# Asking for V on ScalarE's queue, and reading three weight operands in quarters

## Chip, cores and metric

The kernel runs on one core of a Trainium2 chip. The metric is the device time of one execution in microseconds; the figure for a kernel is the median of several runs. A profile is one execution recorded by the hardware profiler. Its span is the time from the first to the last recorded instruction.

The engines are called as in the profile: PE is TensorE (PEld its weight loads), DVE is VectorE, ACT is ScalarE, POOL is GpSimd, SP is SyncE. SPq and ACTq are instructions that the sequencers of SP and ScalarE carry out themselves, above all the issuing of DMAs.

## What is computed

A layer norm feeds two branches: attention over the last 512 positions of a cached K and V, and a gated feed-forward net. The result is `x + s * silu(ffn)`. Cut to what matters, with the shapes filled in:

```python
# x: (1, 2048, 640)   k_cache, v_cache: (1, 32, 2048, 192)   wq: (640, 6144)   wo: (6144, 640)
# w_gate, w_up: (640, 1536)   w_down: (1536, 640)            all bfloat16
def A(xn):                                   # 32 heads of 192, window W = 512
    q = (xn @ wq).reshape(1, 2048, 32, 192).transpose(0, 2, 1, 3)
    k, v = k_cache[:, :, -512:], v_cache[:, :, -512:]
    p = softmax(einsum("bhqd,bhkd->bhqk", q, k) * 192 ** -0.5)
    o = einsum("bhqk,bhkd->bhqd", p, v)
    return o.transpose(0, 2, 1, 3).reshape(1, 2048, 6144) @ wo

def B(xn):
    return (silu(xn @ w_gate) * (xn @ w_up)) @ w_down

xn = layernorm(x)                            # eps 1e-5
return x + A(xn) * silu(B(xn))
```

## The kernel before

It runs in three stages. **The feed-forward net** (0 to about 172 us) works on four blocks of 512 rows. It leaves `silu(B)` in DRAM (`g_d`), and beside it differences of blocks of `wo` (`wo_d`) that the last stage needs. **The attention** (to about 700 us) goes through the 32 heads in 16 pairs, numbered 0 to 15. **The output projection** (to the end) multiplies the attention's output by `wo` in two by two blocks with seven products in place of eight, M1 to M7. Each product needs one weight operand of 1.92 MB, held in a tile `b_w`. M1 and M2 use blocks of `wo` as they are; M7 uses a difference from `wo_d`; `B_SUMS` lists the products whose operands are such differences.

**One pair of heads.** All tiles of the attention hold two heads, one in the lower and one in the upper 64 rows of TensorE. A pair goes through the four blocks of 512 query rows in two halves. Each half is a `scores_phase` and a `stretch`.

- `scores_phase(pr, half)` runs eight steps, n from 0 to 7 in the first half and 8 to 15 in the second. Step n does what `slots` lists for it, then `scores` (six matmuls into a PSUM tile `sc`, and on ScalarE the `exp` that writes the probabilities `p_t`), then `beside(pr, n)`. The slots hold the projection of the queries that are needed next: `differences` ahead of the first scores, `sides` ahead of the second, `across` and `third(0)` ahead of the fourth, `sums` ahead of the fifth, `third(1)` ahead of the seventh, and in the first half `q_diag` ahead of the eighth. `sides` ends with a copy of its PSUM bank to `m_f` on ScalarE; `third(0)` writes into that same bank.
- `stretch(pr, half)` multiplies the probabilities of the half with V (`pv`, 128 matmuls at L689) and divides by the sums (`divide`, on VectorE and ScalarE). After each of four units SP issues a DMA transpose of the result (`OT_b`). `spill` writes these to DRAM in the next half.

The order on each engine is the order of the program, written out by hand: the kernel runs under a manual schedule, and each engine and each DMA queue takes its work as the code names it.

**Loads around a pair.** `beside(pr, n)` places them:

- n = 0: the transpose of the next pair's K by DMA (`transpose_k`, on SP), then `load_v(pr)`, two DMAs of 192 KB on SP, one for each head. They fill `V_p`, of which there is one copy: it can be written once the matmuls of the pair before have read it, and the first `stretch` of this pair needs it.
- n = 10 and 12: the projection weights and K of the pair after next (`load_wq`, `load_k`, on SP).
- n = 4, 5, 12, 13: `spill` of the half before, on SP.
- whatever the table `AHEAD` holds for `(pr, n)`: mostly operands of the output projection, fetched while there is time. `load_b` fetches a weight operand on ScalarE's queue in one DMA, M1 at (1, 10), M7 at (4, 10) and M2 at (7, 10). `wo_part` copies one more operand (M3) within DRAM, in four pieces of 480 KB on SP's queue, at (2, 7), (2, 15), (3, 7) and (3, 15).

`KH` is 24, the number of 128-row chunks of an operand; `pre` is the pool that holds the operands fetched early.

Of the kernel before, what the change touches and what calls it, by code (L numbers as in the profile page):

```python
# [15 lines left out]
def kernel(  # L16
# [13 lines left out]
    nc = tc.nc  # L30
# [20 lines left out]
    KH = NPAIR * PD // P // 2  # L51
# [4 lines left out]
    bf = dt.bfloat16  # L56
# [42 lines left out]
    M1, M7, M2, M5, M6, M4, M3 = PRODUCTS = range(10, 17)  # L99
# [9 lines left out]
    B_SUMS = [m for m in PRODUCTS if len(B_OF[m]) == 2]  # L109
# [3 lines left out]
    wo_d = dram.tile([len(B_SUMS) + 1, P, KH, HC], h16, name="wo_d")  # L113
# [65 lines left out]

    def load_v(pr):  # L180
        for h in range(2):
            nc.sync.dma_start(
                out=V_p[:, :, h, 0:Dh],
                in_=vv[2 * pr + h, k0:Sk, :].rearrange("(p j) d -> p j d", j=KC),
            )
# [41 lines left out]
    a_q, b_w = {}, {}  # L227

    with ExitStack() as fctx:
# [263 lines left out]
        for b in range(NB):  # L493
# [4 lines left out]
            for f in range(NF):  # L498
# [5 lines left out]
                n, phase = divmod((b - 1) * NF + f, 3)  # L504
# [59 lines left out]
    pre = ctx.enter_context(tc.tile_pool(name="out_first", bufs=1, side="right"))  # L564
# [171 lines left out]
    def b_tile(m, pool):  # L736
        return pool.tile([P, KH, HC], h16 if m in B_SUMS else bf, name="b_w", tag="b_w%d" % m)

    def wo_quarter(m, c0=0, c1=KH):
        k, n = B_OF[m][0]  # L740
        return wo[(k * KH + c0) * P : (k * KH + c1) * P, n * HC : (n + 1) * HC].rearrange(
            "(c p) d -> p c d", p=P
        )
# [2 lines left out]

        nc.sync.dma_start(out=wo_d[len(B_SUMS), :, c0:c1, :].bitcast(bf), in_=wo_quarter(M3, c0, c1))

    def load_b(m, pool=None, eng=nc.scalar):
        if m in b_w:  # L750
            pass
        elif pool is None:
            b_w[m] = xc[:, 0:3, :, :].rearrange("p s c n -> p (s c n)").rearrange("p (c d) -> p c d", d=HC)
        else:
            b_w[m] = b_tile(m, pool)[:, :, :]
        if eng is None:
            return
        if m in B_SUMS:
            src = wo_d[B_SUMS.index(m), :, :, :]
        elif m == M3:  # L760
            src = wo_d[len(B_SUMS), :, :, :].bitcast(bf)
        else:
            src = wo_quarter(m)
        eng.dma_start(out=b_w[m], in_=src)

    ROW_PAIRS = [(8 * g + r, 8 * g + 4 + r) for g in range(T // 8) for r in range(4)]

# [154 lines left out]
    def beside(pr, n):  # L922

        b, kc = divmod(n, KC)
        if pr < last:
            if n == 0:
                transpose_k(pr + 1)
            elif b == 2 and kc < 3:
                sum_k(pr + 1, kc)
            elif n >= 11:  # L930
                centre_k(pr + 1, n - 11)
        if n == 0:
            load_v(pr)
        elif pr + 2 < NPAIR and n in (10, 12):
            (load_k if n == 12 else load_wq)(pr + 2)
        half, n8 = divmod(n, 2 * KC)
        prev = pr * NB + 2 * half - 2
        if prev >= 0 and n8 in (4, 5):
            spill(prev + n8 - 4)
        if (pr, n) in AHEAD:  # L940
            what, *args = AHEAD[pr, n]
            what(*args)

    old, middle, most, new = (slice(*ends) for ends in ((0, KH - 6), (KH - 6, KH - 3), (0, KH - 3), (KH - 3, KH)))
    AHEAD = {
        (1, 10): (load_b, M1, pre), (4, 10): (load_b, M7, pre), (7, 10): (load_b, M2, pre),
        (last - 4, 10): (load_a, 0, 2), (last - 3, 10): (load_a, 0, 0),
        (last - 1, 3): (load_a, 0, 3, old), (last - 1, 6): (load_a, 0, 1, old),
        (last - 1, 9): (load_a, 1, 2), (last - 1, 14): (load_b, M5), (last, 5): (load_a, 1, 0),
        (last, 6): (load_a, 0, 3, middle), (last, 7): (load_a, 0, 1, middle),  # L950
    }

    for n in range(4):
        AHEAD[2 + n // 2, (7, 15)[n % 2]] = (wo_part, n * KH // 4, (n + 1) * KH // 4)

    def scores_phase(pr, half):

# [30 lines left out]
    for q in (3, 1):  # L988
        load_a(1, q, most, nc.scalar)
    load_b(M6, wide, None)  # L990
    O_last = wpool.tile([P, 2, 4, 2, Dh], bf, name="O_last", tag="wq_p")
    O_late += [O_last[:, k, :, :, :] for k in range(2)]
# [71 lines left out]
```

## Time and profile before

| | |
|---|---|
| median of 3 runs | 889.05 us (887.2 to 891.53) |
| the profiled execution | 888.36 us |
| its span | 886.6 us |
| granted TensorE clock | 1.00 |
| PE busy | 876.1 us, 99% of the span |
| PEld busy | 581.4 us, 66% |
| DVE busy | 581.4 us, 66% |
| ACT busy | 404.0 us, 46% |
| POOL busy | 113.9 us, 13% |
| DMA, mean rate | 187 GB/s, 165.50 MB |
| packets of SP's queue (q1) | 150.19 MB, 70.4% of 16 engines' span |
| packets of ScalarE's queue (q10) | 13.86 MB, 4.9% |

The shares are of the whole span, and each is an average over three stages. A line of a timeline reads: start, length (both in us from the start of the span), engine, line of the kernel, operation, tile written, tile read, number of instructions merged into the line, and in brackets how long the engine stood idle before it and what it waited for. TensorE's matmuls are pipelined, so a merged line of matmuls is longer than the distance to the next by the length of the pipeline: twelve score matmuls of 0.108 us each start within 1.29 us, and the line shows 1.48.

The issues of V, and the three loads of weight operands in the attention, before:

| transfer | queue | issues | KB each | us from issue to landing, median |
|---|---|---|---|---|
| `V_p` | SP | 32 | 192 | 3.4 |
| `b_w` from `wo` (M1, M2) | ACT | 2 | 1920 | 15.7 |
| `b_w` from `wo_d` (M7 and two later ones) | ACT | 3 | 1920 | 9.4 |
| `wo_d` from `wo` (`wo_part`) | SP | 4 | 480 | 7.0 |

### The profile page before, as it was taken

The page shows a single profiled execution, that of the slowest core. Times are in us where ns is not written, and L with a number is a line of the kernel's source. Part 1 is how long each engine was busy: PE and PEld are TensorE (multiplying, and loading weights), DVE is VectorE, ACT ScalarE, POOL GpSimd, SP SyncE. Part 2 cuts the span into 40 slices and gives each one's busy share as a digit, 9 for nine tenths or more (in the row PEclk, how much of TensorE's full clock was granted, in tenths as well). Part 3 has the DMA queues.
Part 4 walks back from the last instruction along what each step waited for, and adds up shares of the span by engine and source line. Part 5 has one row for each costly group of instructions (what it writes and reads, how often), then busy time and mean ns, then how long its engine had stood idle before and what let it go on. Part 6 is the DMA issues. An engine that isn't in the chain of part 4 may idle for free.

```text
span 886.6 us, 22883 instructions
## 1 busy us (share of the span) xinstructions
PE 876.1 (99%) x9705; PEld 581.4 (66%) x9705; DVE 581.4 (66%) x992; ACT 404.0 (46%) x577; POOL 113.9 (13%) x215
## 2 busy tenths in 40 slices
PE   9999999999999999999999999999999999999998
PEld 5455555567656766766756766766766777777775
DVE  6464766177767877777767777777776457555553
ACT  4222222465756666576666576576667400000000
POOL 0000001012132132122122122122120000000000
PEclk9999999999999999999999999999999999999999
DMA  9659775247989879869889778879799998555410
GB/s 295 175 168 254 206 214 176 66 74 170 229 189 222 181 150 254 157 143 197 204 165 205 149 142 194 181 136 239 153 192 265 249 339 313 200 193 177 173 63 16
DMA packets 272710, 165.50 MB, mean 187 GB/s; under 512 B 174048, under 2 KB 267872, under 8 KB 271968
## 3 DMA queue, kind: packets, MB, share of 16 engines
q1 hardware_dynamic: 264784, 150.19, 70.4%
q10 hardware_dynamic: 7824, 13.86, 4.9%
q8 instruction: 76, 1.25, 0.6%
q14 instruction: 26, 0.21, 0.1%
HBM read 89.95 MB, written 40.24 MB: 147 GB/s over the span
## 4 chain that ended last, share of the span: by engine, by line
PE 97%; DMA 2%; DVE 1%; issue 0%; ACTq 0%; SPq 0%
PE acc L804 21%; PE sc L650 18%; PE mm L596 13%; PE sc L372 11%; PE mm L689 10%; PE sc L689 9%; PE mm L582 8%; PE mm L393 6%; DMA V_p<-in_A_v_cache_dram 1%; PE mm L405 1%; DMA x_t<-in_A_x_dram 1%; PE gu L372 0%; DVE wq_p L174 0%; DVE qT L587 0%; ACTq L249 0%
## 5 line engine op out<-in xcount | busy, mean ns | idle before, releaser
L654 ACT ACTIVATE p_t<-sc 128x1024 bf16<-128x1024 f32 x256 | 253.7, 1024 | 59.9 <-PE sc L650 55.5
L650 PE MATMUL sc<-qT,khat 64*128 64x512 bf16 x1536 | 197.8, 376 | 0.0
L689 PEld LDWEIGHTS <-p_t 64*128 64x128 bf16 x4096 | 172.9, 94 | 14.0 <-DMA V_p<-in_A_v_cache_dram 5.1
L650 PEld LDWEIGHTS <-khat 64*128 64x128 bf16 x1536 | 89.1, 94 | 74.8
L689 PE MATMUL mm<-V_p,p_t 64*128 64x193 bf16 x2112 | 112.2, 243 | 4.3 <-DMA V_p<-in_A_v_cache_dram 4.2
L689 PE MATMUL sc<-V_p,p_t 64*128 64x193 bf16 x1984 | 104.8, 243 | 0.0
L587 DVE TENSOR_REDUCE qT<-mm 128x512 bf16<-128x1024 f32 x66 | 80.6, 1223 | 29.7 <-PE mm L582 27.2
L596 PE MATMUL mm<-xc,wq_p 64*128 64x512 f16 x750 | 94.4, 376 | 0.0
L804 PEld LDWEIGHTS <-a_s 128*128 128x128 f16 x768 | 75.1, 98 | 29.2
L596 PEld LDWEIGHTS <-wq_p 64*128 64x128 f16 (+1 forms) x1050 | 58.7, 94 | 47.6
L634 POOL TENSOR_TENSOR m_f<-m_f 128x1024 f32<-128x1024 f32 x28 | 65.9, 2352 | 178.0 <-DVE qT L629 178.0
L718 ACT ACTIVATE O_b<-sc,r 128x192 bf16<-128x192 f32 x120 | 44.0, 420 | 92.1 <-PE sc L689 84.0
L582 PE MATMUL mm<-xnT,wq_p 64*128 64x512 bf16 x660 | 82.9, 376 | 0.5 <-DVE qT L587 0.5
L804 PE MATMUL acc<-b_w,a_q 128*128 128x320 bf16 (+1 forms) x576 | 81.8, 299 | 0.0
L804 PE MATMUL acc<-b_w,a_s 128*128 128x320 f16 (+1 forms) x576 | 81.8, 299 | 0.0
L804 PEld LDWEIGHTS <-a_q 128*128 128x128 bf16 x576 | 56.3, 98 | 22.1 <-issue 0.3
L854 ACT COPY xc<-acc 128x320 f32<-128x320 f32 x8 | 3.4, 428 | 141.3 <-PE acc L804 130.8
L380 DVE TENSOR_TENSOR hT<-sc,sg 128x512 bf16<-128x512 f32 x46 | 31.6, 688 | 51.9 <-ACT sg L379 51.9
L372 PE MATMUL sc<-xnT,wg_sb 128*128 128x512 bf16 (+1 forms) x260 | 60.2, 354 | 0.5 <-issue 0.3
L582 PEld LDWEIGHTS <-wq_p 64*128 64x128 bf16 x660 | 36.2, 94 | 36.8 <-issue 5.7
L372 PE MATMUL sc<-xnT,wu_sb 128*128 128x512 bf16 (+1 forms) x260 | 60.3, 354 | 0.0
L379 ACT ACTIVATE sg<-sc 128x512 bf16<-128x512 f32 x46 | 27.3, 596 | 68.9 <-PE sc L372 67.4
(83 smaller groups left out, 863.4 us busy)
## 6 DMA issues: line engine op xcount, KB each, us to landing
o_d<-OT_b SPq DMA_DIRECT2D x64, 384.0 KB, 5.8
a_q<-o_d SPq DMA_DIRECT2D x28, 768.0 KB, 6.7
won<-in_A_wo_dram SPq DMA_DIRECT2D x24, 320.0 KB, 4.9
wo_d<-wo_s SPq DMA_DIRECT2D x12, 640.0 KB, 3.9
wq_rows<-in_A_wq_dram SPq DMA_DIRECT2D x16, 480.0 KB, 4.7
wq_rows<-in_A_wq_dram SPq DMA_DIRECT2D x30, 240.0 KB, 6.2
K_p<-in_A_k_cache_dram SPq DMA_DIRECT2D x32, 192.0 KB, 6.3
V_p<-in_A_v_cache_dram SPq DMA_DIRECT2D x32, 192.0 KB, 3.4
```

What stands on the lines that cost most here:

```text
L372: nc.tensor.matmul(out, w_sb[:, c, f * P : (f + 1) * P], xnT[:, c, qc], start=(c == 0), stop=(c == NC - 1),)
L380: nc.vector.tensor_tensor(hTs[b][:, f, :], u, sg[:], ALU.mult)
L393: nc.tensor.matmul(dn[:, n, 0:HC], hTs[b][:, f, rows], wd_sb[:, f, n * HC : (n + 1) * HC], start=(f == 0), stop=(f == NF - 1),)
L582: nc.tensor.matmul(q_ps[:, h, :], w[r, AS_IS[j], c, :], xnT[r, c, b * 512 : (b + 1) * 512], start=(c == 0), stop=(c == NC - 1),)
L587: nc.vector.reduce_sum(q_of(i, j), q_ps[:, :, :].rearrange("p h n -> p n h"), axis=AX.X)
L596: nc.tensor.matmul(ps[:, h, :], ws[h][r, c, :], xs[h][r, c, :], start=(first and c == 0), stop=(c == NC - 1), skip_group_check=True,)
L634: eng.tensor_tensor(m_f[:, SIDE_S, :, :], diag, m_f[:, SIDE_S, :, :], ALU.subtract)
L650: nc.tensor.matmul(sc[:, h, :], khat[r, j, ks], q_of(i, j)[r, :], start=(j == 0), stop=(j == 2))
L654: nc.scalar.activation(p_t[:, :, :], sc[:, :, :], ACT.Exp, scale=scale)
L689: m = nc.tensor.matmul(acc[:, k, h * 256 : h * 256 + Dh + 1], Ps[i][kc][r, h, qt * P : (qt + 1) * P], V_p[r, kc, h, 0 : Dh + 1], start=(p ...
L718: nc.scalar.activation(O_b[:, qt, h, :], a_k[:, h, 0:Dh], ACT.Copy, scale=r[:, k, h, :])
L804: nc.tensor.matmul(ps[k] if ns > 1 else ps, at[:, c, :], b_w[m][:, c, k * w : (k + 1) * w], start=(first and c == 0), stop=(c == KH - 1), ...
```

## The change

Two things change. `load_v` issues its two DMAs on ScalarE's queue. Since `beside` is called after `scores`, they stand there behind the `exp` that writes the pair's first probabilities, and ahead of the copy to `m_f`. And `load_b` takes a range of chunks: M1, M7 and M2 are each read in four pieces of six chunks (480 KB), on SP's queue, at the steps 6 and 14 of two pairs one after the other: M1 in pairs 1 and 2, M7 in pairs 4 and 5, M2 in pairs 7 and 8. The other calls of `load_b` are as before. The same bytes are moved, and the arithmetic is the same.

```diff
     def load_v(pr):
         for h in range(2):
-            nc.sync.dma_start(
+            nc.scalar.dma_start(
                 out=V_p[:, :, h, 0:Dh],
                 in_=vv[2 * pr + h, k0:Sk, :].rearrange("(p j) d -> p j d", j=KC),
             )
...
-    def load_b(m, pool=None, eng=nc.scalar):
+    def load_b(m, pool=None, eng=nc.scalar, c0=0, c1=KH):
...
         if m in B_SUMS:
-            src = wo_d[B_SUMS.index(m), :, :, :]
+            src = wo_d[B_SUMS.index(m), :, c0:c1, :]
         elif m == M3:
-            src = wo_d[len(B_SUMS), :, :, :].bitcast(bf)
+            src = wo_d[len(B_SUMS), :, c0:c1, :].bitcast(bf)
         else:
-            src = wo_quarter(m)
-        eng.dma_start(out=b_w[m], in_=src)
+            src = wo_quarter(m, c0, c1)
+        eng.dma_start(out=b_w[m][:, c0:c1, :], in_=src)
...
     AHEAD = {
-        (1, 10): (load_b, M1, pre), (4, 10): (load_b, M7, pre), (7, 10): (load_b, M2, pre),
...
     for n in range(4):
-        AHEAD[2 + n // 2, (7, 15)[n % 2]] = (wo_part, n * KH // 4, (n + 1) * KH // 4)
+        part = (n * KH // 4, (n + 1) * KH // 4)
+        AHEAD[2 + n // 2, (7, 15)[n % 2]] = (wo_part, *part)
+        for pr, m in ((1, M1), (4, M7), (7, M2)):
+            AHEAD[pr + n // 2, (6, 14)[n % 2]] = (load_b, m, pre, nc.sync, *part)
```

## The prediction

> **What bounds the kernel now.** I read the page's first two parts first (TensorE is 99% busy, the granted clock 9 in all 40 slices, that is 0.9 or more), then the chain that ended last, then the list of waits, then the timeline around the places that they name.
>
> ```profile
> PE 97%; DMA 2%; DVE 1%; issue 0%; ACTq 0%; SPq 0%
> ...
> PEld L689 <- DMA V_p<-in_A_v_cache_dram: 5.1, 3, 2.1
> ...
> PE mm L689 <- DMA V_p<-in_A_v_cache_dram: 4.2, 5, 1.6
> ```
>
> TensorE sets the time from end to end. Whatever delays its stream by x costs x; whatever delays another engine costs nothing until TensorE waits for it. The only DMA for which it waits in the attention is V, in three places. They have to be sized by the stream itself, since the two rows overlap and one place can count twice. The first matmul of a half pair (L596, `differences`) starts at 205.94, 222.96, 238.94, 258.33, 274.31, 291.33 and so on: halves that open a pair take 17.02 us, the others 15.98, to within 0.01, in all but three cases. These three take 19.39 (from 238.94), 18.57 (from 340.31) and 18.50 (from 440.87). The excess is 2.37 + 1.55 + 1.48 = **5.40 us**, all that V costs before.
>
> Why it is late there: SP's queue at the start of pair 2 (start, length, both in us).
>
> ```profile
> 237.09 10.07 SPq L721 DMA_TRANSPOSE OT_b<-O_b  x4
> 247.53 1.27 SPq L192 DMA_TRANSPOSE KT<-K_p  x1
> 248.90 1.72 SPq L182 DMA_DIRECT2D V_p<-in_A_v_cache_dram  x2
> ```
>
> V stands on SP behind four transposes of the half before and the transpose of K. In most pairs these four take 5.6 to 6.7 us, and V is asked for 5.4 us into pair 3 (279.72 against 274.31). In pairs 2, 5 and 8 they take 8.4 to 10.1 us, since `load_b` put 1.92 MB into the DMA engines at 227.81, 329.95 and 429.29, 10 to 12 us before each of these pairs. V is then asked for 9.3 to 10 us into the pair, and it is needed at 11.7 (286.00 in pair 3). The first matmul with V of pair 2 starts at 252.39, after 1.58 us of idle time put down to V.
>
> **The change, removed.** V goes past SP's five transposes and is asked for behind the first probabilities, 1.94 us into the pair (276.25 against 274.31). Landing takes 3.1 to 4.4 us in all 32 issues, and the second issue would stand at 2.7 us, so V would be there at 5.8 to 7.1, with 4.6 us to spare before 11.7. Both edits act on the same 5.40 us, which is counted once. Gain: **5.40 us**, bounds 0 (the waits stay) and 5.40.
>
> **Moved to SP.** `load_b` becomes 12 issues of 480 KB instead of three. Nearest row: `wo_part`, 480 KB on the same queue, 0.69 to 2.47 us of SP each. V's two issues (1.24 to 1.72 us) leave SP in each pair. What stands behind the pieces on SP is the transposes, K, wq and the spills. Cover: K^T is needed by VectorE at L200 in the second half, and even in pair 2, where the four transposes took 4 us longer, nothing but V stopped TensorE. The `wo_part` of 480 KB at 267.44, 282.53 and 300.98 went by with halves of 17.02 and 15.98 behind them. New is that in pair 2 a `wo_part` follows a piece directly (positions 6 and 7, 14 and 15), 960 KB, half of the load that did the harm. Taken as 0; without cover, one more late V as in pair 2, 2.4 us. The three issues that leave ScalarE (0.34 to 0.39 us each) were hidden: the probabilities after them start where they do in other pairs. 0.
>
> **Added to ScalarE.** This is the cost. The timeline of the start of pair 3 is below. Two DMA issues now stand between the first probabilities and the copy `m_f` (L626), in pairs 1 to 15. Pair 0 has another order there, with ScalarE idle 0.55 us before its second probabilities.
>
> ```profile
> 276.03 1.26 PE L596 MATMUL mm<-xnT,wq_p 64*128 64x512 bf16 x10
> ...
> 276.25 1.02 ACT L654 ACTIVATE p_t<-sc 128x1024 bf16<-128x1024 f32 x1
> ...
> 277.11 1.48 PE L650 MATMUL sc<-qT,khat 64*128 64x512 bf16 x12
> ...
> 277.38 1.01 ACT L626 COPY m_f<-mm 128x1024 f32<-128x1024 f32 x1
> ...
> 278.45 1.26 PE L582 MATMUL mm<-xnT,wq_p 64*128 64x512 bf16 x10
> ```
>
> The copy empties the bank of `sides`; `third(0)` (L582) writes that bank next. The copy ends at 277.38 + 1.01 = 278.39, `third(0)` starts at 278.45, and the scores ahead of it are through at 277.11 + 1.29 = 278.40. So TensorE has no slack at all here. Every delay of the copy moves `third(0)`, behind it the third scores, then the rest of the pair. The copy starts 1.13 us after the probabilities. What goes into this gap, by rows of ScalarE (ACTq: its DMA issues) and of SP:
>
> ```profile
> 667.64 1.02 ACT L654 ACTIVATE p_t<-sc 128x1024 bf16<-128x1024 f32 x1 [0.44 <-PE sc L650]
> 667.67 0.33 ACTq L764 DMA_DIRECT2D xc<-wo_d  x1
> ...
> 679.51 1.24 SPq L182 DMA_DIRECT2D V_p<-in_A_v_cache_dram  x2
> ...
> 712.30 0.33 ACTq L764 DMA_DIRECT2D b_w<-wo_d  x1
> 712.67 0.43 ACT L854 COPY xc<-acc 128x320 f32<-128x320 f32 x1 [10.55 <-DMA OT_b<-O_last]
> ```
>
> A DMA issue starts 0.03 us after the probabilities in front of it (667.67 against 667.64), while they run. Work behind an issue starts 0.04 us after its end (712.63 to 712.67): ScalarE keeps the order, though that copy's matmuls had ended 9 us earlier. A semaphore step adds some 0.05 us on either side (SP shows 0.09 between V's two issues). V's two issues themselves have no row on ScalarE. From below: its two `a_q` issues in a row, 684.34 to 685.20, 0.86 us. From above: V behind a K transpose on SP, 1.72 us. In between: V alone on SP in the last pair, where no K transpose precedes it, 0.575 + 0.09 + 0.575 = 1.24 us. I take that one, same bytes and same pattern; the two engines issue alike (`a_q<-o_d` at least 0.319 us on SP, 0.333 on ScalarE). Then 0.03 + 0.05 + 1.24 + 0.05 + 0.04 = 1.41, less 1.13 = **0.28 us per pair, 15 pairs, 4.2 us**. By the low row 1.03, under 1.13: 0. By the high row 1.89: 0.76 per pair, 11.4 us. Behind the issues on ScalarE there is nothing else that is short of time: it is busy 11 of 17 us in such a half.
>
> **Sum.** The profiled execution took 888.36 us (span 886.6, 1.8 around it), 0.69 below the median of 889.05. 888.36 - 5.40 + 4.2 = 887.2; against the median, 889.05 - 1.2 = **887.9 us**.
>
> **Rivals.** *All gain, no cost.* The issues fit into the 1.13 us: 889.05 - 5.4 = 883.7. For it: every plain issue on ScalarE behind the start-up took 0.33 to 0.44 us. Against it: all 32 issues of V took at least 0.575 on SP, also the unhindered ones, so that this looks like the price of its pattern. [...]
>
> *The issue is held up by SP's transposes.* This is the rival on the slower side. When ScalarE asks for V (276.3), SP is issuing transposes back to back until 279.63. Behind such a run SP's own issue of V took 0.81 to 1.04 us in most pairs instead of 0.575, and in pair 4 a `load_b` on ScalarE started at 329.95, 1.3 us after the scores of the probabilities before it had ended (328.62), while SP was issuing. If ScalarE pays as SP did, 0.76 us per pair: 889.05 - 5.4 + 11.4 = 895.1. It turns slower by over 0.5% from (5.4 + 4.45) / 15 = 0.66 us per pair. Against it: issues at 227.81 and 429.29 kept to 0.385 us beside SP's loads. [...] No run here shows an issue on ScalarE during transposes.
>
> *The change doesn't do what it says.* V is still late because the pieces crowd the engines for longer; the DMA share reached 1.1 to 1.2 from 232 to 242. Then the cost stays and the gain goes: 889.05 + 4.2 = 893.3. Against it: no half was longer where V followed a 480 KB `wo_part` (267.44), and there are 4.6 us to spare.
>
> **Chances.** Forecast 0.46, no cost 0.17, held up 0.27, V still late 0.10. 0.5% is 4.45 us, about what a measurement of this kernel can tell from no change (its three runs lie 0.5% apart). Faster by that needs under 0.06 us per pair: 0.17, all from the first rival. Slower: 0.25 of the second and 0.04 of the third, 0.29. Within: 0.54. The range reaches from the full gain, 883.5, to the second rival with a little room, 896.0; a few longer holds as at 329.95 would lie beyond. The forecast's own range is 885.5 (0.12 us per pair) to 892 (0.56).
>
> **What would show it.** No half pair longer than 18 us, and no wait of L689 for V: the gain is right. The halves that open a pair at 17.3 instead of 17.02: the cost is right; 17.0 is the first rival, 17.7 and above the second. The copy `m_f` starting 1.4 us after the first probabilities, right behind V's second issue, and a wait of TensorE at L582: the mechanism is right. The prediction is wrong in kind if TensorE stops at another place, or if halves that ask for no V change.

## The result, and the profile after

The changed kernel took **896.63 us** (median of 9 runs, 892.48 to 898.33); the kernel before took 891.24 beside it (9 runs). The ratio is **1.0062, 95% interval 1.0045 to 1.008**: slower by some 5.5 us. Put on the earlier median of 889.05 this is 894.6. (The quotient of two medians can differ from a ratio given here by 0.001.) The profiled execution took 893.75 us with a span of 892.0, at a granted clock of 1.00 as before; the span is 5.4 longer.

First the page of the changed kernel: the shares of the chain that ended last, by engine.

```profile
PE 90%; DMA 4%; ACT 2%; ACTq 2%; DVE 1%; issue 1%; SPq 0%
```

ScalarE and its DMA issues now stand on the chain (ACT 2%, ACTq 2%; before, ACT was not among them), and TensorE's own share fell from 97% to 90%. The list of waits says for what it waits (total us, times, longest):

```profile
PEld L582 <- issue: 16.3, 31, 2.6
...
PE mm L582 <- ACT m_f L626: 8.0, 12, 2.3
```

Before, L582 waited 5.7 us behind "issue" and not at all for `m_f`. The waits of L689 for V are gone. The start of pair 3 shows how it comes about (start, length, engine, instruction, and in brackets the idle time before it):

```profile
275.08 1.26 PE L596 MATMUL mm<-xnT,wq_p 64*128 64x512 bf16 x10
...
275.29 1.02 ACT L654 ACTIVATE p_t<-sc 128x1024 bf16<-128x1024 f32 x1
275.30 1.44 ACTq L182 DMA_DIRECT2D V_p<-in_A_v_cache_dram  x2
...
276.16 1.47 PE L650 MATMUL sc<-qT,khat 64*128 64x512 bf16 x12
...
276.83 1.01 ACT L626 COPY m_f<-mm 128x1024 f32<-128x1024 f32 x1 [0.52 <-PE mm L596]
277.90 1.26 PE L582 MATMUL mm<-xnT,wq_p 64*128 64x512 bf16 x10 [0.27 <-ACT m_f L626]
```

The copy starts 0.09 us after V's second issue has ended, 1.54 us after the first probabilities (1.13 before), and L582 waits for it. That is the mechanism of the prediction. Its size is not. The opening halves of the pairs 1 to 14 take 17.29 to 18.32 us. Over the undisturbed 17.02 they have 8.13 us too much, summed. Pair 15 needs 2.47 us more than before from its first matmul to the first scores behind V (13.75 for 11.28). The other halves stay at 15.98. With the gain of 5.40 and pair 1 starting 0.31 later, -5.40 + 8.13 + 2.47 + 0.31 = 5.5, and the spans differ by 5.4. So V's two issues on ScalarE cost **10.6 us, 0.71 per pair**, where 0.28 was forecast.

The first issue is not the trouble. It took 0.55 to 0.56 us and began 0.01 to 0.06 us behind the probabilities in all 15 pairs. The second one differs from pair to pair:

| pair | begins behind the end of the first, us | length, us | the DMA ahead of it on its semaphore landed before it, us | an issue of SP began before it, us | half too long, us |
|---|---|---|---|---|---|
| 1 | 0.09 | 0.94 | 0.94 | 0.09 | 0.61 |
| 2 | 0.10 | 0.82 | 0.17 | 0.03 | 0.49 |
| 3 | **0.34** | 0.55 | **0.02** | 1.09 | 0.41 |
| 4 | 0.10 | 1.15 | 0.40 | 0.09 | 0.82 |
| 5 | 0.10 | 0.59 | 0.54 | 1.21 | 0.27 |
| 6 | **0.17** | 0.55 | **0.02** | 0.55 | 0.31 |
| 7 | 0.09 | 1.63 | 1.71 | 0.09 | 1.30 |
| 8 | **0.82** | 0.56 | **0.02** | 0.61 | 0.96 |
| 9 | 0.10 | 0.97 | 0.53 | 0.09 | 0.64 |
| 10 | 0.10 | 0.76 | 1.73 | 0.09 | 0.43 |
| 11 | 0.09 | 0.61 | 1.41 | 1.11 | 0.28 |
| 12 | 0.10 | 1.18 | 0.38 | 0.08 | 0.85 |
| 13 | **0.34** | 0.56 | **0.02** | 1.25 | 0.48 |
| 14 | 0.10 | 0.60 | 0.31 | 1.05 | 0.28 |
| 15 | **2.39** | 0.58 | **0.02** | 0.28 | 2.47 |

Two kinds of disturbance are in this table. In some pairs the issue begins late but is short (3, 6, 8, 13, 15). In others it begins at once but is long (1, 2, 4, 7, 9, 10, 12). In 5, 11 and 14 there is hardly either: 0.59 to 0.61 us, begun at once.

### The profile page after: what moved, and what is told of

Same layout as the page of the kernel before. It is cut to its first block, busy times and chain, and to the rows that moved or that the text cites. A ratio compares the mean times of both kernels' runs of the same rounds, so it can differ in the third digit from the quotient of the medians.

```text
span 892.0 us, 22893 instructions
## 1 busy us (share of the span) xinstructions
PE 875.9 (98%) x9688; PEld 581.7 (65%) x9705; DVE 581.4 (65%) x992; ACT 403.8 (45%) x577; POOL 113.7 (13%) x215
## 3 DMA queue, kind: packets, MB, share of 16 engines
q8 instruction: 76, 1.25, 0.6%
## 4 chain that ended last, share of the span: by engine, by line
PE 90%; DMA 4%; ACT 2%; ACTq 2%; DVE 1%; issue 1%; SPq 0%
PE acc L804 20%; PE sc L650 16%; PE sc L372 11%; PE mm L596 10%; PE mm L689 9%; PE sc L689 8%; PE mm L582 8%; PE mm L393 6%; DMA OT_b<-O_b 3%; ACT m_f L626 2%; ACTq L182 1%; PE mm L405 1%; DMA o_d<-OT_b 1%; DMA x_t<-in_A_x_dram 1%; DVE O_b L712 0%
## 5 line engine op out<-in xcount | busy, mean ns | idle before, releaser
L689 PEld LDWEIGHTS <-p_t 64*128 64x128 bf16 x4096 | 173.1, 94 | 8.4
L689 PE MATMUL mm<-V_p,p_t 64*128 64x193 bf16 x2112 | 111.7, 243 | 0.0
L689 PE MATMUL sc<-V_p,p_t 64*128 64x193 bf16 x1984 | 104.8, 243 | 0.0
L582 PE MATMUL mm<-xnT,wq_p 64*128 64x512 bf16 x660 | 82.9, 376 | 8.8 <-ACT m_f L626 8.0
L582 PEld LDWEIGHTS <-wq_p 64*128 64x128 bf16 x660 | 36.2, 94 | 47.3 <-issue 16.3
L629 DVE TENSOR_TENSOR qT<-mm,m_f 128x1024 bf16<-128x1024 f32 x30 | 36.7, 1225 | 42.1 <-ACT m_f L626 42.1
```

The source lines that it names most:

```text
L582: nc.tensor.matmul(q_ps[:, h, :], w[r, AS_IS[j], c, :], xnT[r, c, b * 512 : (b + 1) * 512], start=(c == 0), stop=(c == NC - 1),)
L629: nc.vector.tensor_tensor(q_pair(i)[:, 1:4:2, :], st["ps"][:, :, :], m_f[:, SIDE_S, ::-1, :], ALU.add)
L689: m = nc.tensor.matmul(acc[:, k, h * 256 : h * 256 + Dh + 1], Ps[i][kc][r, h, qt * P : (qt + 1) * P], V_p[r, kc, h, 0 : Dh + 1], start=(p ...
```

## The experiments

Each kernel is the changed one (or the one before) with one edit. Ratios are against runs of the kernel before on the same chip. The theories at the start: **theory 1**, any DMA issue of ScalarE is held up by SP's transposes; **theory 2**, the second of two issues in a row costs by itself. **Theory 3** was formed once the plain copy below had been seen: ScalarE can hand over one DMA at once, and the next waits until the first is taken up, which stands behind SP's transposes. **Theory 4** was formed later and is told where it arose.

**One part alone: the quarters.** V stays on SP.

```diff
     def load_v(pr):
-            nc.scalar.dma_start(
+            nc.sync.dma_start(
```

> Only the quarters of M1, M7 and M2 on SP; V on SP as before. Both theories of ScalarE's cost (theory 1: V's second issue is held up while SP issues the fourth transpose of the half before; theory 2: two issues in a row on ScalarE cost this by themselves) have nothing to act on here: the halves that open a pair take 17.02 us again in pairs 1 to 15. If the quarters alone take the crowding away, V is asked for 5.4 to 6.5 us into pairs 2, 5 and 8, no wait for V is left, and the time is 5.4 us under before (ratio 0.994). If V's place on ScalarE was needed for that, pairs 2, 5 and 8 keep some of their 1.5 to 2.4 us of excess and the ratio is 0.997 to 1.000.

Measured: 883.46 against 889.55 us, ratio 0.9932 (0.9917 to 0.9947). All opening halves are 17.02 or 17.03, the last 11.28. (Its span of 882.5 is 4.1 shorter and not 5.4, since its attention reached pair 1 1.4 us later.) SP's queue at the start of pair 2:

```profile
238.46 6.46 SPq L721 DMA_TRANSPOSE OT_b<-O_b  x4
244.97 2.05 SPq L192 DMA_TRANSPOSE KT<-K_p  x1
247.12 1.25 SPq L182 DMA_DIRECT2D V_p<-in_A_v_cache_dram  x2
```

The four transposes take 6.46 us instead of 10.07, and V is asked for 6.8 us into the pair, in time. **The quarters alone bring the whole gain**; this version beats both kernels.

**The other part alone: V on ScalarE**, with the operands in one DMA each.

```diff
     def load_v(pr):
-            nc.sync.dma_start(
+            nc.scalar.dma_start(
```

> Only V on ScalarE; the three operands in one piece as before. If V's place alone cures the late V: no wait of TensorE for V, and the opening halves are longer by 0.3 to 1.3 us as in the changed kernel, 10.6 us in all, so 5 us over before (ratio 1.006). If the quarters were needed: waits for V stay in pairs 2, 5 and 8 and the ratio is up to 1.012. Theory 1 expects the excess to be largest in pairs 2, 5 and 8, where the transposes take longer; theory 2 expects the same excess in all pairs.

Measured: ratio 1.0227 (1.0206 to 1.0249), far beyond the 1.012 expected at most. Halves of 23.49, 19.93 and 22.33 in the pairs 2, 5 and 8, the pairs of `load_b`, and 17.32 to 18.05 elsewhere. TensorE never waits for V. ScalarE in pair 2:

```profile
241.78 1.02 ACT L654 ACTIVATE p_t<-sc 128x1024 bf16<-128x1024 f32 x1
243.74 3.85 ACTq L182 DMA_DIRECT2D V_p<-in_A_v_cache_dram  x2
247.69 1.01 ACT L626 COPY m_f<-mm 128x1024 f32<-128x1024 f32 x1 [4.88 <-DMA V_p<-in_A_v_cache_dram]
```

Here even the first issue is late, by 1.9 us. M1 was issued at 228.46 and landed 15.3 us later, at 243.72. At the time I read this as SP's crowded transposes holding ScalarE. It is the first sign of theory 4.

**V later in the pair**, at step 3, where SP issues no transposes of O.

```diff
-        if n == 0:
+        if n == 3:
             load_v(pr)
```

> The changed kernel with both issues of V on ScalarE behind the fourth probabilities (step 3) in place of the first, some 6.2 us into the pair, when SP's transposes are over. V's second issue stands at 6.9 us and lands 2.9 to 4.4 us later, 9.8 to 11.3, before 11.7. Theory 1 (held up by SP's transposes): both issues take 0.55 to 0.6 us and the second follows within 0.1 us; the opening halves take 17.02 to 17.1 us; 5 us under before (ratio 0.994 to 0.995). Theory 2 (the second of two issues costs by itself): the second issue takes or waits 0.55 to 1.6 us here too, in the same spread, although ScalarE has 0.7 us of slack here, and the opening halves take 17.0 to 17.5.

Measured: ratio 1.0048 (1.0031 to 1.0065), a miss. The copy is on time, but V is now late: it landed a median of 4.8 us after its issue, and my 4 us were too short. The start of V's matmuls in pair 8:

```profile
451.67 0.51 PE L689 MATMUL mm<-V_p,p_t 64*128 64x193 bf16 x8
453.05 0.51 PE L689 MATMUL mm<-V_p,p_t 64*128 64x193 bf16 x8 [0.87 <-DMA V_p<-in_A_v_cache_dram]
```

The eight matmuls of the first head begin, those of the second head wait: the second of two issues sets the time. **Step 1**, the same edit with `n == 1`:

> The changed kernel with V's two issues one step later on ScalarE, behind the copy m_f and the second probabilities (step 1), 4 us into the pair. V would land at 8 to 9.5 us, ahead of 11.7, so no wait for V. Theory 1: the fourth transpose is over (3.8 us into the pair in the kernel before) and only K's transpose can hold an issue; what a hold delays is the third probabilities, which have some 0.6 us of slack, so the opening halves take 17.02 with a few at 17.1 to 17.6; ratio 0.993 to 0.996. Theory 2: two issues cost by themselves, but behind the copy that slack hides most; second issues scatter from 0.55 to 1.6 us as in the changed kernel.

Measured: ratio 0.998 (0.9966 to 0.9995), short of the 0.993 to 0.996 of theory 1. Halves of 17.02, but 18.79 in pair 2, where the second issue took 2.11 us, and 14.25 in the last, where the first issue came 3.2 us after the probabilities ahead of it.

**One DMA for both heads**, at step 0, with the quarters.

```diff
-        for h in range(2):
-            nc.scalar.dma_start(
-                out=V_p[:, :, h, 0:Dh],
-                in_=vv[2 * pr + h, k0:Sk, :].rearrange("(p j) d -> p j d", j=KC),
-            )
+        nc.scalar.dma_start(
+            out=V_p[:, :, :, 0:Dh],
+            in_=vv[2 * pr : 2 * pr + 2, k0:Sk, :].rearrange("h (p j) d -> p j h d", j=KC),
+        )
```

> The changed kernel with V of both heads in one DMA of 384 KB on ScalarE behind the first probabilities. One issue of 0.55 to 0.6 us fits into the 1.13 us ahead of the copy m_f. Theory 1: the first issue mostly fell between two transposes (0.55 us in all pairs), so the copy starts 1.13 to 1.2 us after the probabilities, with a few pairs held up where a transpose is in the way; ratio 0.994 to 0.997. Theory 2: no second issue, no cost at all, 17.02 in all pairs; ratio 0.994. If the cost goes by bytes or descriptors of V and not by issues, the one issue takes 1.2 us or more and the ratio is 1.000 or above.

Measured: 884.23 against 889.55, ratio 0.9936 (0.9923 to 0.995). Every opening half is 17.02. ScalarE and SP at the start of pair 3:

```profile
275.09 1.02 ACT L653 ACTIVATE p_t<-sc 128x1024 bf16<-128x1024 f32 x1
275.15 0.62 ACTq L181 DMA_DIRECT2D V_p<-in_A_v_cache_dram  x1
276.22 1.01 ACT L625 COPY m_f<-mm 128x1024 f32<-128x1024 f32 x1
```

```profile
271.29 6.88 SPq L720 DMA_TRANSPOSE OT_b<-O_b  x4
```

The issue takes 0.62 us in the midst of SP's transposes (0.61 to 0.63 in the pairs 1 to 15), and the copy keeps its 1.13 us. Theory 1 falls: here ScalarE issued beside transposes at no cost.

**Is it K's transpose?** It stands on SP directly behind those of O; here it moves to step 5.

```diff
-            if n == 0:
-                transpose_k(pr + 1)
-            elif b == 2 and kc < 3:
+            if b == 2 and kc < 3:
...
+        if pr < last and n == 5:
+            transpose_k(pr + 1)
```

> The changed kernel with the transpose of the next pair's K issued at step 5, behind the spills, instead of step 0. It is the control for the next run: of SP's transposes only the last two of the half before are left beside V's issues. Theory 1 (SP's transposes hold V's second issue): most of the holds come from the fourth transpose of O, which stays, so the opening halves of pairs 1 to 14 keep most of their excess (0.3 to 1.3 us, 8.1 us in all before), ratio 1.000 to 1.006; were it K's transpose that holds, the excess falls to 0.28 us a pair, ratio 0.998. Theory 2 (the second of two issues in a row costs by itself): no change, ratio 1.006.

Measured: 1.0054 (1.0035 to 1.0073), halves of 17.30 to 18.38: as before. **Then the last transpose of O too**, as a plain copy (which leaves the output of these blocks untransposed):

```diff
+        if i < last * NB and i % NB == 3 and q2 == 1:
+            nc.sync.dma_start(
+                out=OT_b[:, 6 * q2 : 6 * q2 + 6, :].rearrange("p c q -> p (c q)"),
+                in_=O_b[:, 2 * q2 : 2 * q2 + 2, :, :].rearrange("p t h d -> p (t h d)"),
+            )
+            return
```

> As the run before, and the fourth DMA transpose of every pair's second half is replaced by a plain copy of the same 192 KB between the same tiles (in these blocks the output is left untransposed); SP then issues no transpose while ScalarE issues V's second head. Theory 1: V's second issue takes 0.55 to 0.65 us in every pair and follows the first by 0.1 us; the copy m_f starts 1.35 to 1.45 us after the probabilities, the opening halves take 17.25 to 17.35 us, which is the price of two issues alone (0.2 to 0.3 us a pair, 3 to 4.5 us); ratio 0.998 to 0.999. Theory 2: the second issue still takes or waits up to 1.6 us in a third of the pairs and the halves scatter from 17.3 to 18.3; ratio 1.004 to 1.006.

Measured: 1.0037 (1.0019 to 1.0056), halves of 17.29 to 18.95. The long issues stay, now beside a plain DMA of SP. In pair 7 the issues of SP, above, and ScalarE, below, finish together (413.43 and 413.47):

```profile
411.64 1.79 SPq L722 DMA_DIRECT2D OT_b<-O_b  x1
```

```profile
411.02 2.45 ACTq L182 DMA_DIRECT2D V_p<-in_A_v_cache_dram  x2
```

So this long issue had no transpose beside it, only another issue of SP at the same moment. This is what led to theory 3.

**The two heads at different steps**: one issue at step 0, one at step 1.

```diff
-        if n == 0:
-            load_v(pr)
+        if n < 2:
+            load_v(pr, (n,))
```

> The changed kernel with V's first head asked for at step 0 and its second at step 1, both on ScalarE, so that the copy m_f and the second probabilities stand between the two issues. Theory 3 (formed after the runs before: ScalarE can hand over one DMA at once; the next waits until the first is taken up, and that stands behind SP's transposes): each issue takes 0.55 to 0.6 us, the copy starts 1.13 to 1.2 us after the first probabilities, the opening halves take 17.02 in nearly all pairs, with pair 15 longer by up to 3 us because M5's 1.92 MB go ahead on ScalarE's own queue; ratio 0.994 to 0.997. Theory 1 (any issue of ScalarE that meets a transpose is held): the second issue meets K's transpose and is held 0.2 to 1.5 us in many pairs, as the issues of V did; what is left after slack is 17.0 to 17.6; ratio 0.997 to 1.000.

Measured: 1.0007 (0.9994 to 1.002), where theory 3 expected 0.994 to 0.997. All issues take 0.55 to 0.59 us: apart from each other, none was long. The second one still begins late in four: pair 1 (by 0.5 us, which costs nothing), pair 2 (half of 17.81), pair 14 (17.86), and the last (16.39), where the second head is issued 4.4 us behind the probabilities. Theory 3 has no reason for these.

**One DMA, and a tiny second one** (4 bytes for each of 128 partitions) behind it.

```diff
+        nc.scalar.dma_start(out=act_t[:, :].bitcast(bf), in_=x2[0:P, 0:2])
```

> The kernel with V in one DMA on ScalarE (0.9936), and right behind it a second issue on ScalarE that moves 4 bytes to each of 128 partitions (of x into act_t, which nothing reads). Theory 3: the second issue is held as V's second head was, 0.4 us of its own plus 0 to 1.2 us until V is taken up; the copy starts 1.2 to 2.4 us after the probabilities and the opening halves take 17.1 to 18.3; ratio 0.998 to 1.004. If V's bytes or descriptors cost and not the second issue: 0.61 + 0.09 + 0.35 to 0.4 us just fit into the 1.13 us, 17.02 to 17.1 in all pairs; ratio 0.994.

Measured: 1.012 (1.01 to 1.014), halves of 17.47 to 18.48, more than the 1.004 expected at most. So it is the second issue, not V's bytes. In pair 7 these 512 bytes hold ScalarE for 1.61 us:

```profile
412.82 0.61 ACTq L181 DMA_DIRECT2D V_p<-in_A_v_cache_dram  x1
413.53 1.61 ACTq L185 DMA_DIRECT2D act_t<-in_A_x_dram  x1
415.24 1.01 ACT L626 COPY m_f<-mm 128x1024 f32<-128x1024 f32 x1 [1.45 <-PE sc L650]
```

**One DMA, operands whole**: the kernel before with this edit alone.

```diff
-        for h in range(2):
-            nc.sync.dma_start(
-                out=V_p[:, :, h, 0:Dh],
-                in_=vv[2 * pr + h, k0:Sk, :].rearrange("(p j) d -> p j d", j=KC),
-            )
+        nc.scalar.dma_start(
+            out=V_p[:, :, :, 0:Dh],
+            in_=vv[2 * pr : 2 * pr + 2, k0:Sk, :].rearrange("h (p j) d -> p j h d", j=KC),
+        )
```

> The kernel before with V in one DMA on ScalarE behind the first probabilities; M1, M7 and M2 stay whole on ScalarE's queue. If the quarters are needed also with one issue: in pairs 2, 5 and 8 the issue of V is held while the 1.92 MB drain (the first issue started 1.9 us late in pair 2 and 2.7 in pair 8 with two issues), these pairs' opening halves take 18 to 20 us, the others 17.02; ratio 0.996 to 1.002. If one issue is all that matters: 17.02 in all pairs, ratio 0.994.

Measured: 1.0004 (0.9991 to 1.0018). Halves of 19.03 and 19.47 in pairs 2 and 8, else 17.02. The first lines below are ScalarE at the start of pair 2, the last is from the DMA issues around 229.5 (KB, us to landing):

```profile
242.75 1.02 ACT L653 ACTIVATE p_t<-sc 128x1024 bf16<-128x1024 f32 x1
245.17 0.61 ACTq L181 DMA_DIRECT2D V_p<-in_A_v_cache_dram  x1
245.88 1.01 ACT L625 COPY m_f<-mm 128x1024 f32<-128x1024 f32 x1 [2.11 <-DMA b_w<-in_A_wo_dram]
```

```profile
b_w<-in_A_wo_dram ACTq DMA_DIRECT2D x1, 1920.0 KB, 15.7
```

V is asked for 2.4 us late, though it is alone, and the copy behind it is put down to M1's DMA. M1 was issued at 229.45; 229.45 + 15.7 = 245.15. V's issue begins 0.02 us behind that landing.

**M5 on SP.** In pair 15 the changed kernel loses 2.47 us; M5's 1.92 MB had been issued on ScalarE shortly before.

```diff
-        (last - 1, 14): (load_b, M5),
+        (last - 1, 14): (load_b, M5, None, nc.sync),
```

> The changed kernel with M5, the one operand still read whole (1.92 MB, behind the seventh probabilities of pair 14's second half), on SP's queue in place of ScalarE's. It asks why pair 15 loses 2.5 us, much more than the others. If V's second issue stands there behind M5 on ScalarE's own queue: the stretch from pair 15's first matmul to its first scores behind V, 13.75 us in the changed kernel and 11.28 before, falls to 11.3 to 12.1, and the rest stays (opening halves 8 us too long together); ratio about 1.003. If it is the crowding by 1.92 MB, whichever queue brings them (SP's transposes take 7 to 8 us there and V's second issue waits for them): 13 us and more, ratio about 1.006.

Measured: 1.0046 (1.003 to 1.0063); pair 15 loses 0.92 instead of 2.47, between the two expectations. The other opening halves lose 9.4 in all instead of 8.1, above all pair 13 (1.57 instead of 0.49), so not all of the gain in pair 15 is left. The reason for pair 15 is below.

**Theory 4.** The releaser "DMA b_w" led to the semaphores. The trace says on which semaphore each DMA counts, and on which one an issue waits (V's second issue in pair 8 counts on 104 and waits on 104). In the changed kernel the 523 DMAs of SP and ScalarE count on **eight semaphores**, 65 or 66 on each, in turn: in 424 of the 522 steps from one issue to the next the semaphore is the next of the eight numbers (in the kernel before, with 514 DMAs, in 498 of 513). The trace has all the landings too, so that each issue can be set against the landing of the DMA ahead of it on the same semaphore, here called its holder. Of the 515 that have one, **none begins before its holder has landed**; the shortest distance is 0.02 us. The fourth column of the table of pairs shows this distance for V's second issue. Counted by time of issue, the holder stands eight places ahead in 309 of the 515, and 3 to 13 in the others. Ahead of V's second issue it is the first transpose of O, four or five places ahead. In all five late pairs the issue begins 0.02 us after this transpose has landed. Pair 8 of the changed kernel, SP's queue, ScalarE, and the DMA issue at 439.59 with its time to landing:

```profile
439.59 6.02 SPq L721 DMA_TRANSPOSE OT_b<-O_b  x4
```

```profile
443.44 1.93 ACTq L182 DMA_DIRECT2D V_p<-in_A_v_cache_dram  x2
445.47 1.01 ACT L626 COPY m_f<-mm 128x1024 f32<-128x1024 f32 x1 [1.07 <-PE sc L650]
```

```profile
OT_b<-O_b SPq DMA_TRANSPOSE x1, 5.2
```

439.59 + 5.2 = 444.79, and the second issue began at 444.81. The bracket of the copy names the scores, which had long been there; a wait inside the queue of DMA issues is not named in a timeline. The chain that ended last does name it. Over these microseconds it reads (start, length, what):

```profile
439.59 5.20 DMA OT_b<-O_b
444.79 0.02 issue
444.81 0.56 ACTq L182
...
445.47 1.02 ACT m_f L626
```

In the changed kernel `DMA OT_b<-O_b` holds 25.0 us of the chain, and none before; it stands on the page, among the lines of the chain, at 3%. Read there, the landing of a transpose would have been the first suspect. The same distance is found at the other late starts. With M5 on SP the first transpose of pair 15 landed after 5.2 us instead of 6.7, and V's second issue came at 680.40 instead of 681.25. V on ScalarE with whole operands waits for M1 and M2 in the pairs 2 and 8, and in pair 5 its second issue waits for a transpose. The DMA of 512 bytes behind the one DMA of V waited in the same way in 7 of 15 pairs, 0.02 us behind a transpose; in the other 8 it began at once and took 0.70 to 1.68 us, where the late ones took 0.34 to 0.37. With the heads at different steps, the late second issues of pairs 1, 2, 14 and 15 each begin 0.02 us behind the landing of a transpose. The one DMA of both heads shows no such wait: in pair 3 it began 0.06 us behind the probabilities (275.15 against 275.09), and no opening half was longer than 17.02.

Two more runs to test it. **One more DMA on SP**, so that the holder is the second transpose:

```diff
         if n == 0:
+            if 0 < pr < last:
+                nc.sync.dma_start(out=act_t[:, :].bitcast(bf), in_=x2[0:P, 0:2])
             load_v(pr)
```

> The changed kernel with one more DMA in pairs 1 to 14: 4 bytes for each of 128 partitions, on SP, behind the transpose of K and ahead of V; nothing reads what it brings there. Theory 4, formed on the traces so far: the program gives the DMAs of SP and ScalarE eight completion semaphores in turn, and a DMA is not issued before the one eight places ahead of it has landed. For V's second issue that is the first of the four transposes of O: in pairs 3, 6, 8, 13 and 15 of the changed kernel it started 0.02 us after this one had landed. With one more DMA between, it is the second transpose, which landed at 210.5, 243.1, 277.0, 311.0, 343.5, 377.5, 409.6, 445.4, 479.8, 511.7, 545.4, 580.2, 613.2, 646.1. Theory 4 expects V's second issue to start 0.02 us after the second transpose has landed, in nearly all of pairs 1 to 14, to take 0.55 us there, and to end 9 us later in sum than in the changed kernel: ratio 1.013 to 1.019. Theory 3 (ScalarE can hand over one DMA, the next waits until it is taken up) expects the second issue where it was, and 1.004 to 1.008.

Measured: 904.46 against 891.72, ratio **1.0154 (1.0132 to 1.0176)**, as theory 4 says. In 8 of the 14 pairs V's second issue begins 0.02 us after the second transpose has landed, in 3 more 0.07 to 0.08; in pairs 4, 7 and 10 that landing was past, and the issue begins at once and is long (0.79 to 1.82). ScalarE in pair 9:

```profile
481.04 1.02 ACT L654 ACTIVATE p_t<-sc 128x1024 bf16<-128x1024 f32 x1
481.10 2.90 ACTq L182 DMA_DIRECT2D V_p<-in_A_v_cache_dram  x2
484.10 1.01 ACT L626 COPY m_f<-mm 128x1024 f32<-128x1024 f32 x1 [2.04 <-DMA OT_b<-O_b]
```

The second transpose, issued at 478.82, landed 4.6 us later, at 483.43; the second issue began at 483.45. One tiny DMA on another engine's queue, which nothing reads, cost 0.9% here by shifting who waits for whom.

**Fewer DMAs between**, so that the holder is no transpose:

```diff
-        if prev >= 0 and n8 in (4, 5):
+        if prev >= 0 and (n8 == 4 or n8 == 5 and not (n == 5 and pr < last - 1)):
             spill(prev + n8 - 4)
+        if 0 < pr < last - 1 and n == 9:
+            spill(pr * NB - 1)
...
-        AHEAD[2 + n // 2, (7, 15)[n % 2]] = (wo_part, *part)
+        AHEAD[2 + n // 2, (9, 15)[n % 2]] = (wo_part, *part)
-            AHEAD[pr + n // 2, (6, 14)[n % 2]] = (load_b, m, pre, nc.sync, *part)
+            AHEAD[pr + n // 2, (8, 14)[n % 2]] = (load_b, m, pre, nc.sync, *part)
```

> The changed kernel with the second spill of a pair's first half, the pieces of step 6 and the parts of step 7 moved to steps 8 and 9, in pairs 1 to 13, so that there are fewer DMAs between the first transpose of O and V. The DMA eight places ahead of V's second issue is then a spill or a piece that has long landed; in pairs 14 and 15 it is a transpose as before. Theory 4 expects V's second issue within 0.15 us of the end of the first in all of pairs 1 to 13, where it was 0.17 to 0.82 us behind it in pairs 3, 6, 8 and 13 of the changed kernel; issues that are longer than 0.62 us remain, since those had nothing to wait for by a semaphore: opening halves of 17.3 to 18.4, ratio 1.002 to 1.007. Theory 3 expects late starts of the second issue as before, in four or five of the pairs 1 to 13. If both the late starts and the long issues go, the long ones come of the semaphores too, and the halves are 17.3 throughout, ratio 0.998 to 1.001.

Measured: 904.37, ratio 1.0153 (1.0125 to 1.0181), far from the 1.002 to 1.007 expected. The holders were not long landed: the spills and pieces that took the transposes' place now landed later still. In pair 3 V waits for a piece of M1, landed at 279.04, and for a part of M3:

```profile
275.44 1.02 ACT L654 ACTIVATE p_t<-sc 128x1024 bf16<-128x1024 f32 x1
279.06 2.08 ACTq L182 DMA_DIRECT2D V_p<-in_A_v_cache_dram  x2
281.24 1.01 ACT L626 COPY m_f<-mm 128x1024 f32<-128x1024 f32 x1 [4.77 <-DMA wo_d<-in_A_wo_dram]
```

The first issue, which had never been late in the changed kernel, is 3.6 us late. The forecast of the time failed; what it shows is the same wait again, with other holders: V's first issue, at 279.06, comes 0.02 us behind the landing at 279.04.

**What is left for theory 3.** Seven of these kernels, the changed one among them, issue V twice in a row at step 0. In their 105 pairs, 52 second issues began over 0.12 us behind the first, 50 of them within 0.1 us after a landing for which they had to wait; the other two (V alone on ScalarE, pairs 3 and 14, 0.39 and 0.53 us behind the first) stay unexplained. The remaining 53 began at once. Of these, 34 came within 0.2 us behind the start of an issue on SP (30 transposes, 4 plain copies), and all 34 were long, 0.76 to 1.82 us; of the other 19, 16 took 0.58 to 0.65. First issues took at most 0.60 us, whatever SP did. So at step 0 a second issue right behind a first was long when SP had just begun one too. That does not hold for every issue of SP: with V at step 3, three of four second issues that began so shortly behind a spill's issue took 0.59 to 0.61 us, and the 2.11 us of step 1 began 1.09 us behind a transpose of K. What makes it long is not seen in these traces.

## Why the prediction was wrong

- **What bounds the kernel; the gain of 5.40 us.** Right. No half waits for V any more, and the quarters alone keep all opening halves at 17.02.
- **"V goes past SP's five transposes" and so is in time.** Right in what it says, but not needed: with quarters V is in time behind them.
- **Moved to SP, 0.** Right. The halves that ask for no V are 15.98 throughout.
- **Added to ScalarE.** The step that failed. The mechanism was as forecast: the copy right behind V's second issue, and TensorE stopped at L582. The term of the sum was 0.28 us per pair and 4.2 in all; measured are 0.71 and 10.6. It left out two waits: the second issue's wait for the landing of an earlier DMA, and the stretch of a second issue beside one of SP. Two undisturbed issues are worth 0.06 + 0.55 + 0.09 + 0.55 + 0.09 - 1.13 = 0.21 to 0.22 us per pair, 3.3 in all, a little under the forecast. On top come the late starts, 3.7 us over the 15 pairs (the second column of the table less 0.09), and the long issues, 3.8 us (the length less 0.55). Together 10.8, against 10.6 on TensorE. The price was taken from V's two issues on SP in the last pair, "same bytes and same pattern". But the row showed two issues that had nothing to wait for, and on ScalarE their neighbours are others.
- **The rival on the slower side** came nearest: 0.76 us per pair, 11.4 in all, 895.1. Its price was near, its mechanism in part wrong. SP's transposes did not hold up an issue of ScalarE as such (0.61 to 0.63 us for the one DMA of both heads beside them). Of what comes on top of two undisturbed issues, one half, 3.7 us, is the wait for a transpose to land; the other, 3.8 us, is two issues in a row beside one of SP. That 0.76, taken from SP's own issues, comes so near to 0.71 is in good part luck.
- **A row that was misread.** The prediction cited `load_b` in pair 4 of the kernel before, at 329.95, as a hold "while SP was issuing", and set 227.81 and 429.29 against it, since those issues were short. The list of DMA issues of the kernel before, for the third transpose on SP, issued at 325.58:

```profile
OT_b<-O_b SPq DMA_TRANSPOSE x1, 4.4
```

It landed at 329.93, and `load_b` began 0.02 us later. The issue at 227.81 came 0.02 us behind a landing too, the one at 429.29 not until 0.44 us behind. Their lengths, 0.34 us at 329.95 and 0.39 us at the other two, told nothing of a wait; their starts did. The trace of before held it, and I read lengths.
- **The copy behind the issues.** The first rival needed both issues to fit into 1.13 us. The copy never started before the second issue had ended. In 14 of 15 pairs it started 0.10 us after it, in pair 15 0.04, and so 1.40 to 3.56 us after the probabilities.

## What to carry to other kernels

Before pricing a moved DMA issue at the length of an undisturbed one, look up in the trace which DMA is ahead of it on its semaphore, and when that one lands: here V's second issue, 0.55 us long when undisturbed, stood 0.02 us behind such a landing in five of 15 pairs, and began up to 2.39 us behind the first. ScalarE's work is short of time at step 0, and there one DMA for both operands (0.9936) was worth more than a later place for both (0.998 at step 1, 1.0048 at step 3) or for one of two (1.0007). And where two edits aim at the same loss, try each alone: here the quarters gave all of the 0.7%, and the move of V took it back twice over.

## What was not expected

- A DMA of 512 bytes on SP, which nothing reads, made the changed kernel slower by a further 0.9% (1.0154 against 1.0062), and one of 512 bytes on ScalarE cost 1.8% (1.012 against 0.9936). Neither moved any bytes to speak of.
- A DMA issue on ScalarE beside a running chain of transposes cost nothing extra: 0.61 to 0.63 us in 15 of 15 pairs. In the changed kernel two in a row, without any wait for a landing, held ScalarE for up to 2.3 us (pair 7: 0.55 + 0.10 + 1.63).
- The size of the loads showed twice. With whole operands SP's four transposes at the start of pair 2 took 10.07 us, with quarters 6.46. And with V on ScalarE, in two DMAs or in one, a whole M1 landed 15.3 and 15.7 us after its issue, and V in pair 2 was issued 0.02 us after that landing, 1.9 and 2.4 us late.
